# Chunk attention in front of a gated MLP on one core: norms moved behind PV, and PV and scores put in one place from unit 12

## The chip, the cores and the metric

The kernel runs on one core of a Trainium2 chip. The metric is the device time of one execution in microseconds (us); smaller is better. The time of a kernel is the median of several executions; one further view of it is a profiled execution, from which all rows of the profile come.

## The reference

```
q, k, v: (8, 8, 576, 64)  batch, heads, sequence, head_dim;  chunks of 64 positions
scores = q_c @ k_c.T / sqrt(64)             within each chunk of 64 alone
attn   = softmax(scores)
x      = (attn @ v_c) as (4608, 512)         tokens x (heads * head_dim)
h      = x @ w_in                            (4608, 2048)
out    = (h * sigmoid(beta * h)) @ w_out     (4608, 512), float32
```

## The kernel before

**Units and blocks.** The 4608 tokens are cut into 18 units of 256 tokens (two halves `s` of 128), and two units make one of nine blocks of 512 tokens, numbered 0 to 8. Attention works on units, the MLP on blocks. The kernel is one long list of instructions that is written out in the order in which each engine will run its share; nothing reorders it afterwards. Each engine runs its own instructions in that order and waits at one whose inputs or buffers aren't ready.

**The steps of a unit** u, with the lines of the profile:
- loads of q, k and v by GpSimd's DMA queue (L99, L113). The load of unit u + 4 is issued with T of unit u (`loads_to`), and waits until the buffers of unit u (four each for q and k) are free.
- `emit_T`: for units from 8 on, two DMA transposes on SP (L152), of k and then of q, into kT and qT, two buffers each.
- `emit_sc`: 32 small matmuls (64 x 64, L225) make the scores in the PSUM pool ps_s (one tile of two banks); ACT makes the exponential et (L231).
- `emit_pv`: for each half 16 small matmuls (64 x 65, L266), with a column of ones that gives the sum. Where they go is the argument `where`: "x" is the pool ps_x (one tile of two banks), "s" is ps_s, "p" two of the four banks of ps_p (the tiles called y).
- `emit_norm`: reciprocal (L285) and product (L287) on DVE, into x in 16 bits; for "p" in two parts.
- `emit_xt_dma`: one DMA transpose on SP (L318) into the xt tile of the block, which has three buffers. The first big matmul of a block needs all four transposes of its two units.

**The steps of a block** j: `emit_m` for m = 0 to 15: four matmuls of 128 x 512 (hps, L329) into one bank of ps_p, a tanh on ACT (sg, L339), and a product on DVE (gt, L343). `emit_t` for four tiles t of 128 tokens: 16 matmuls (ops, L361) into one bank of ps_p, in two halves of eight, then a copy on ACT (osb, L371) and the output by SP's DMA queue (L373). The four banks of ps_p are given out in turn to hps, ops and y tiles.

**The order.** For blocks 3 to 8 the order is made from a list of items with a position in the block (0 to 1) and a priority, and sorted by both. The m of block j stand at 0.02 + 0.061 m, the halves of t of block j - 1 at multiples of 0.1225, and between them the attention of the next block's units 2j + 2 and 2j + 3. There are two ways to place attention. Units below MU = 14 come through `att_items`: scores, T of the next unit, PV and the two norms stand at places of their own, in 0.43 of a block. Units from MU on come as a "hop": PV of the unit (its second half into ps_p), the scores of the next unit, T of the unit after that, and the norms with their transposes, all in one place. The scores of unit MU itself stand at 0.89 of the block before its hop.

Of the kernel before, what the change touches and what calls it, by code (L numbers as in the profile page):

```python
# [15 lines left out]
def kernel(  # L16
# [54 lines left out]
    blocks = [(u, 2) for u in range(0, NU, 2)]  # L71
    NB = len(blocks)
    XU = 8
    MU = 14
    unit_block = {}
    for j, (u0, n) in enumerate(blocks):
        for u in range(u0, u0 + n):
# [138 lines left out]
    def emit_sc(u, split=False, later=False):  # L216
        qt, kt = qT.pop(u), kT.pop(u)
        sc = ps_s.tile([128, 2, H, CH], FP32, tag="s", name="sc")
        if u >= XU:
            qx, kx = (t.rearrange("p h s e -> p (h s e)").rearrange("p (j c t) -> p j c t", j=H, c=2)  # L220
                      for t in (qt, kt))
            for jj in range(H):
                for par in range(2):
                    for c in range(2):
                        nc.tensor.matmul(  # L225
                            out=sc[64 * c:64 * c + 64, par, jj, :],
                            lhsT=kx[64 * par:64 * par + 64, jj, c, :],
                            rhs=qx[64 * par:64 * par + 64, jj, c, :],
                        )
            et = et_p.tile([128, 2, H, CH], FP16, tag="et", name="et")  # L230
            nc.scalar.activation(out=et, in_=sc, func=ACTF.Exp, scale=scale)  # L231
            et_t[u] = et
            return
        for h in range(H):
            for e in range(2):
                for c in range(4):
                    p0, o0 = 32 * c, 64 * (c % 2)
                    nc.tensor.matmul(  # L238
                        out=sc[o0:o0 + 64, c // 2, h, :],
                        lhsT=kt[p0:p0 + 32, h, :, e],  # L240
                        rhs=qt[p0:p0 + 32, h, :, e],
                        start=(e == 0),
                        stop=(e == 1),
                    )
        et = et_p.tile([128, 2, H, CH], FP16, tag="et", name="et")
        ex_t[u] = [
            lambda s=s: nc.scalar.activation(out=et[:, s], in_=sc[:, s], func=ACTF.Exp, scale=scale)  # L247
            for s in ([0, 1] if split or later else [slice(0, 2)])
        ]
        et_t[u] = et  # L250
        while ex_t[u] and not later:
            emit_ex(u)

    def emit_pv(u, where=("x", "s")):
        et = et_t.pop(u)
        for s in (1, 0) if u >= MU else (0, 1):
            i = 2 * u + s
# [17 lines left out]
    def emit_norms(u):  # L275
        for s in (1, 0) if u >= MU else (0, 1):
            emit_norm(u, s)
            emit_xt_dma(u, s)

    def emit_norm(u, s):  # L280
        x = x_t.pop((u, s))
        rd = rd_p.tile([128, 2, 4, 1], FP32, tag="rd", name="rd")
        x16 = x_p.tile([128, 2, 4, D], FP16, tag="x16", name="x16")
        for r, z in [(slice(0, 2), x[0])] if len(x) == 1 else list(enumerate(x)):
            nc.vector.reciprocal(out=rd[:, r], in_=z[..., D:D + 1])  # L285
            o = x16[:, r]
            nc.vector.tensor_tensor(  # L287
                out=o, in0=z[..., 0:D], in1=rd[:, r].to_broadcast(list(o.shape)), op=ALU.mult
            )
        x16_t[u, s] = x16  # L290
# [25 lines left out]
    def emit_xt_dma(u, s):  # L316
        xf = x16_t.pop((u, s)).rearrange("p r h d -> p (r h d)")
        nc.sync.dma_start_transpose(out=xt_at(u, s), in_=xf)  # L318
# [3 lines left out]
    def emit_m(j, m, c0=0, n=None, later=False):  # L322
        n = blocks[j][1] * UNIT if n is None else n
        if j not in gt_t:
            gt_t[j] = gt_p.tile([128, KFF, 512], FP16, tag="gt", name="gt")
        hps = ps_p.tile([128, 512], FP32, tag="p", name="hps")
        xr = xt_t[j].rearrange("p t (r k) (c q) -> p (t r) (k c) q", r=2, c=2)
        for kk in range(KDM):
            nc.tensor.matmul(  # L329
                out=hps[:, 0:n],  # L330
                lhsT=w_in16[m // 2][:, kk, (m % 2) * 128:(m % 2) * 128 + 128],
                rhs=xr[:, c0 // CH:(c0 + n) // CH, 2 * (kk % 2) + kk // 2, :],
                start=(kk == 0),
                stop=(kk == KDM - 1),
            )
        sg = sg_p.tile([128, 512], FP32, tag="sg", name="sg")

        def act():
            nc.scalar.activation(  # L339
                out=sg[:, 0:n], in_=hps[:, 0:n], func=ACTF.Tanh, scale=beta2[:, m:m + 1])  # L340

        def vec():
            nc.vector.scalar_tensor_tensor(  # L343
                out=gt_t[j][:, m, c0:c0 + n], in0=sg[:, 0:n], scalar=1.0, in1=hps[:, 0:n],
                op0=ALU.add, op1=ALU.mult,
            )

        if later:
            return act, vec
        act()  # L350
        vec()
# [3 lines left out]
    def emit_t(j, t, k0=0, k1=None):  # L355
        k1 = KFF if k1 is None else k1
        if k0 == 0:
            ops_t[j, t] = ps_p.tile([128, DM], FP32, tag="p", name="ops")
        ops = ops_t[j, t]
        for kk in range(k0, k1):  # L360
            nc.tensor.matmul(  # L361
                out=ops,
                lhsT=gt_t[j][:, kk, t * 128:(t + 1) * 128],
                rhs=w_out16[kk // 4][:, kk % 4, :],
                start=(kk == 0),
                stop=(kk == KFF - 1),
            )
        if k1 < KFF:
            return
        osb = osb_p.tile([128, DM], FP32, tag="osb", name="osb")  # L370
        nc.scalar.activation(out=osb, in_=ops, func=ACTF.Copy, scale=0.5)  # L371
        r0 = blocks[j][0] * UNIT + t * 128
        nc.sync.dma_start(out=out[r0:r0 + 128, :], in_=osb)  # L373
# [20 lines left out]
    with tc.manual_schedule():  # L394
# [74 lines left out]
        for i in range(16):  # L469
# [11 lines left out]
            if i == 15:  # L481
                a0, v0 = emit_m(1, 0, 0, 256, True)
# [74 lines left out]

        def att_items(u, a0, w):
            return [(a0, 2, ("sc", u)), (a0 + 0.40 * w, 3, ("pv", u)),
                    (a0 + 0.41 * w, 3, ("norm", u, 0)), (a0 + 0.55 * w, 3, ("norm", u, 1)),  # L560
                    (a0 + 0.10 * w, 3, ("T", u + 1))]

        for j in range(3, NB):
            items = [(0.02 + 0.98 * m / KFF, 0, ("m", m)) for m in range(KFF)]
            for t in range(4):
                for hf in range(2):
                    items.append((0.98 * (t + 0.5 * hf) / 4, 1, ("t", t, hf)))
            if 2 * j + 2 < MU:
                for i in range(2):
                    items += att_items(2 * j + 2 + i, 0.03 + 0.43 * i, 0.43)  # L570
                if 2 * j + 4 == MU:
                    items += [(0.89, 2, ("sc", MU)), (0.90, 3, ("T", MU + 1))]
            elif j + 1 < NB:
                for i in range(2):
                    items.append((0.15 + 0.5 * i, 2, ("hop", 2 * j + 2 + i)))
            items.sort(key=lambda it: it[:2])
            for _, _, it in items:
                if it[0] == "m":
                    emit_m(j, it[1])
                elif it[0] == "t":  # L580
                    emit_t(j - 1, it[1], 8 * it[2], 8 * it[2] + 8)
                elif it[0] == "sc":
                    emit_sc(it[1])
                elif it[0] == "pv":
                    emit_pv(it[1])
                elif it[0] == "hop":
                    emit_pv(it[1], ("x", "p" if it[1] + 1 < NU else "s"))
                    if it[1] + 1 < NU:
                        emit_sc(it[1] + 1)
                    if it[1] + 2 < NU:  # L590
                        emit_T(it[1] + 2)
                    emit_norms(it[1])
                elif it[0] == "norm":
                    emit_norm(it[1], it[2])
                    emit_xt_dma(it[1], it[2])
                elif it[1] < NU:
                    emit_T(it[1])
# [49 lines left out]
```

## Time and profile before

| | |
|---|---|
| median of 5 runs | 288.44 us (288.24, 288.29, 288.44, 289.51, 290.15) |
| profiled execution | 289.51 us, of which the span from first to last instruction is 287.7 |
| TensorE clock granted | 0.999 |
| busy: TensorE, ACT, DVE, GpSimd | 98%, 51%, 49%, 33% |
| big matmuls, hps (L329) and ops (L361) | 44% and 42% of the chain that ended last |
| transposes xt (L318), issue to landing | 2.4 to 7.3 us, median 3.5 |

Rows give the start, the duration, the engine, the line of the kernel and what is written and read (out<-in). A number in brackets is the idle time of the engine just before, with what ended it. "PEld" is TensorE's weight load, "SPq" an instruction that SP issues to its DMA queue. In the chain that ended last each piece follows on what released it; "issue" is time in which the engine waited for nothing that the profile shows.

### The profile page before, as it was taken

To read this page: it belongs to the slowest core of one execution; us is meant where nothing else is said; L and a number is where in the kernel's file an instruction comes from. 1 tells how busy PE (TensorE), PEld (TensorE's weight loads), DVE (VectorE), ACT (ScalarE), POOL (GpSimd) and SP (SyncE) were. 2 spreads that over 40 slices of the span, in tenths; PEclk is the share of its full clock that TensorE was granted. 3 is DMA by queue.
4 is the path that set the end of the run, shared out by engine and by line. 5 is a ranking of instruction groups with operands and counts; after the bars stand their busy time and mean duration, and the time that the engine had idled before them with its cause. 6 is when DMAs were issued, how large, how long until landed. Compare 5 with 4: busy or idle time off the path is not lost.

```text
span 287.7 us, 6664 instructions
## 1 busy us (share of the span) xinstructions
PE 280.6 (98%) x2779; PEld 136.2 (47%) x2779; DVE 141.9 (49%) x260; ACT 146.0 (51%) x223; POOL 95.7 (33%) x125
## 2 busy tenths in 40 slices
PE   6989999999999999999999999999999999999995
PEld 3464456544544444444444444444444444444444
DVE  3587533776558554535453445454544545333300
ACT  4377218773557545454544454554545444444411
POOL 8853677578073991243542600000000000000000
PEclk9999999999999999999999999999999999999999
DMA  8999999999999999999999992555451212010012
GB/s 198 177 197 206 181 179 210 209 161 152 198 100 175 177 176 179 131 173 114 174 147 170 132 191 60 127 76 127 57 129 39 73 39 73 36 39 36 36 73 75
DMA packets 141086, 37.40 MB, mean 130 GB/s; under 512 B 128001, under 2 KB 136577, under 8 KB 141057
## 3 DMA queue, kind: packets, MB, share of 16 engines
q0 software_dynamic: 99136, 17.83, 80.5%
q1 hardware_dynamic: 41776, 19.09, 30.8%
q8 instruction: 22, 0.36, 0.5%
q10 hardware_dynamic: 144, 0.07, 0.1%
q14 instruction: 8, 0.06, 0.1%
HBM read 36.71 MB, written 9.44 MB: 160 GB/s over the span
## 4 chain that ended last, share of the span: by engine, by line
PE 96%; POOL 1%; ACT 1%; issue 1%; DVE 0%; DVEq 0%; POOLq 0%
PE hps L329 44%; PE ops L361 42%; PE warm L381 2%; PE x L266 2%; PE sc L238 1%; PE sc L225 1%; PE ops L603 1%; ACT xt L304 1%; POOL h L401 1%; PE sc L198 1%; POOL vbig L113 1%; PE xp L303 0%; ACT et L208 0%; PE y L266 0%; PE xp L311 0%
## 5 line engine op out<-in xcount | busy, mean ns | idle before, releaser
L343 DVE SCALAR_TENSOR_TENSOR gt<-sg,hps 128x512 f16<-128x512 f32 (+1 forms) x153 | 99.2, 655 | 107.8 <-ACT sg L339 107.5
L329 PE MATMUL hps<-xt,win 128*128 128x512 f16 (+1 forms) x612 | 136.9, 367 | 1.3 <-ACT xt L304 0.7
L339 ACT ACTIVATE sg<-hps,beta 128x512 f32<-128x512 f32 (+1 forms) x153 | 100.4, 663 | 73.6 <-PE hps L329 73.5
L361 PE MATMUL ops<-wout,gt 128*128 128x512 f16 x560 | 131.1, 379 | 0.0
L329 PEld LDWEIGHTS <-win 128*128 128x128 f16 x612 | 58.0, 98 | 62.9 <-issue 2.0
L361 PEld LDWEIGHTS <-gt 128*128 128x128 f16 x560 | 54.0, 98 | 63.7
L371 ACT ACTIVATE osb<-ops 128x512 f32<-128x512 f32 x35 | 20.9, 598 | 42.5 <-PE ops L361 42.5
L113 POOL DMA_DIRECT2D vbig<-in_v_dram x40 | 34.3, 877 | 11.1 <-DMA wout<-in_moe_w_out_dram 3.2
L99 POOL DMA_DIRECT2D qu<-in_q_dram x22 | 18.8, 871 | 36.8 <-DMA qT<-qu 34.0
L287 DVE TENSOR_TENSOR x<-x,rd 128x512 f16<-128x512 f32 x31 | 21.4, 692 | 1.2
L99 POOL DMA_DIRECT2D ku<-in_k_dram x22 | 18.9, 889 | 0.0
L285 DVE RECIPROCAL rd<-x 128x8 f32<-128x8 f32 x31 | 6.2, 200 | 13.5 <-PE x L266 13.5
L247 ACT ACTIVATE et<-sc 128x1024 f16<-128x1024 f32 (+1 forms) x8 | 6.4, 811 | 8.7 <-PE sc L238 8.7
L231 ACT ACTIVATE et<-sc 128x1024 f16<-128x1024 f32 x10 | 10.2, 1018 | 0.2
L266 PEld LDWEIGHTS <-et 64*64 64x64 f16 x576 | 6.0, 107 | 7.4 <-issue 3.8
L381 PE MATMUL warm<-idle 128*128 128x512 f16 (+1 forms) x32 | 8.7, 425 | 0.0
L105 POOL DMA_DIRECT2D qu<-in_q_dram x9 | 6.8, 768 | 2.2 <-DMA win<-in_moe_w_in_dram 1.5
L266 PE MATMUL x<-vbig,et 64*64 64x65 f16 x496 | 7.3, 194 | 0.2 <-ACT et L208 0.2
L105 POOL DMA_DIRECT2D ku<-in_k_dram x9 | 6.8, 759 | 2.2 <-DMA win<-in_moe_w_in_dram 1.3
L615 DVE TENSOR_SCALAR osb<-ops 128x256 f32<-128x256 f32 (+1 forms) x2 | 0.7, 358 | 12.1 <-PE ops L603 12.1
L131 POOL DMA_DIRECT2D win<-in_moe_w_in_dram x8 | 6.0, 761 | 1.1 <-DMA vbig<-in_v_dram 1.1
L179 DVE STREAM_TRANSPOSE t<-h 128x512 f32<-128x512 f32 (+1 forms) x5 | 4.1, 905 | 3.3 <-ACT h L178 3.3
(46 smaller groups left out, 72.5 us busy)
## 6 DMA issues: line engine op xcount, KB each, us to landing
out_dram<-osb SPq DMA_DIRECT2D x35, 256.0 KB, 2.9
vbig<-in_v_dram POOLq DMA_DIRECT2D x32, 128.0 KB, 7.1
qu<-in_q_dram POOLq DMA_DIRECT2D x20, 128.0 KB, 4.9
ku<-in_k_dram POOLq DMA_DIRECT2D x20, 128.0 KB, 5.8
win<-in_moe_w_in_dram POOLq DMA_DIRECT2D x8, 256.0 KB, 8.7
wout<-in_moe_w_out_dram POOLq DMA_DIRECT2D x4, 512.0 KB, 12.7
qu<-in_q_dram POOLq DMA_DIRECT2D x3, 256.0 KB, 7.3
ku<-in_k_dram POOLq DMA_DIRECT2D x3, 256.0 KB, 7.8
```

The source lines that it names most:

```text
L99: nc.gpsimd.dma_start(out=tv[off:off + n, sp], in_=src[b, :, s:s + n, :].rearrange("h p d -> p h d"),)
L105: nc.gpsimd.dma_start(out=t[off // 2:(off + n) // 2], in_=src[b, :, s:s + n, :].rearrange("h (p r) d -> p h r d", r=2),)
L113: nc.gpsimd.dma_start(out=vbig[off:off + n, i, :, 0:D], in_=v[b, :, s:s + n, :].rearrange("h p d -> p h d"),)
L231: nc.scalar.activation(out=et, in_=sc, func=ACTF.Exp, scale=scale)
L266: nc.tensor.matmul(out=(x[0][64 * c:64 * c + 64, r, g, 0:D + 1] if len(x) == 1 else x[r][64 * c:64 * c + 64, g, 0:D + 1]), lhsT=(et[64 * r ...
L287: nc.vector.tensor_tensor(out=o, in0=z[..., 0:D], in1=rd[:, r].to_broadcast(list(o.shape)), op=ALU.mult)
L329: nc.tensor.matmul(out=hps[:, 0:n], lhsT=w_in16[m // 2][:, kk, (m % 2) * 128:(m % 2) * 128 + 128], rhs=xr[:, c0 // CH:(c0 + n) // CH, 2 * ...
L339: nc.scalar.activation(out=sg[:, 0:n], in_=hps[:, 0:n], func=ACTF.Tanh, scale=beta2[:, m:m + 1])
L343: nc.vector.scalar_tensor_tensor(out=gt_t[j][:, m, c0:c0 + n], in0=sg[:, 0:n], scalar=1.0, in1=hps[:, 0:n], op0=ALU.add, op1=ALU.mult,)
L361: nc.tensor.matmul(out=ops, lhsT=gt_t[j][:, kk, t * 128:(t + 1) * 128], rhs=w_out16[kk // 4][:, kk % 4, :], start=(kk == 0), stop=(kk == K ...
L371: nc.scalar.activation(out=osb, in_=ops, func=ACTF.Copy, scale=0.5)
L381: nc.tensor.matmul(out=d[:, 0:w], lhsT=idle[:, 0:128], rhs=idle[:, 0:w])
```

## The change

The norms of a unit below MU, and with them their xt transposes, now stand right behind its PV, both at the same position (before: the first just behind PV, the second 0.06 of a block later). MU is 12 instead of 14, so units 12 and 13 come as hops in block 5, and the scores of unit 12 and T of unit 13 stand at the end of block 4. The two hops of a block stand at 0.22 and 0.68 instead of 0.15 and 0.65. In `emit_pv` and `emit_norms` the halves of units from MU on go in the order 1, 0; this now holds for units 12 and 13 too.

```diff
-    MU = 14
+    MU = 12
...
             return [(a0, 2, ("sc", u)), (a0 + 0.40 * w, 3, ("pv", u)),
-                    (a0 + 0.41 * w, 3, ("norm", u, 0)), (a0 + 0.55 * w, 3, ("norm", u, 1)),
+                    (a0 + 0.40 * w, 4, ("norm", u, 0)), (a0 + 0.40 * w, 5, ("norm", u, 1)),
                     (a0 + 0.10 * w, 3, ("T", u + 1))]
...
-                    items.append((0.15 + 0.5 * i, 2, ("hop", 2 * j + 2 + i)))
+                    items.append((0.22 + 0.46 * i, 2, ("hop", 2 * j + 2 + i)))
```

In the list of each engine this does the following. On TensorE the scores of unit 12 stand between m 14 and m 15 of block 4 (before: between m 0 and m 1 of block 5); in block 5 there are two places with small matmuls instead of five; the first hop of blocks 5, 6 and 7 stands between m 3 and t 1 (before, in blocks 6 and 7: between m 2 and m 3), the second between m 10 and m 11 as before. On DVE the two norms of units 8 to 11 stand next to each other, ahead of the gt of the m that follows the PV (before: one m's gt ahead of the first, one between them). On SP the order is the same up to unit 12, and then T of 14 and 15 stand ahead of the xt transposes of 12 and 13. GpSimd's list is the same.

## The prediction

> **What bounds the kernel now.** I read the page's busy line first, then the waits of TensorE, then the chain in order of time around the blocks that are edited, and last the transposes there.
>
> ```profile
> PE 280.6 (98%) x2779; PEld 136.2 (47%) x2779; DVE 141.9 (49%) x260; ACT 146.0 (51%) x223; POOL 95.7 (33%) x125
> ```
>
> ```profile
> PE hps L329 <- issue: 0.5, 1, 0.5
> ```
>
> TensorE is busy 98% of the span, and DVE and ACT half of it. Behind the start, TensorE waits once, for 0.5 us. So an edit of order can gain only what lies between the big matmuls. The chain shows this price:
>
> ```profile
> 127.11 0.38 PE sc L225 x32
> 127.48 0.97 PE hps L329 x4
> ...
> 131.04 0.38 PE x L266 x32
> 131.42 0.97 PE hps L329 x4
> ...
> 154.07 1.73 PE ops L361 x8
> 155.80 0.50 issue
> 156.30 1.02 PE hps L329 x4
> ...
> 190.81 0.25 PE y L266 x16
> 191.19 0.32 PE sc L225 x32
> 191.50 0.97 PE hps L329 x4
> ...
> 242.90 1.73 PE ops L361 x8
> ...
> 270.53 10.36 PE ops L361 x48
> ```
>
> From 242.90 to 270.53 there are sixteen pieces of eight matmuls (8 pairs of m, 8 halves of t) and nothing else: 27.63 us is the bare block. Four hps matmuls are 0.86 us there; behind a small group they are 0.97.
>
> The 0.50 us at 155.80 is the first m of block 5. It needs the xt tile of block 5, the last piece of which is the second transpose of unit 11:
>
> ```profile
> L318 SPq DMA_TRANSPOSE xt<-x x1: 1190/1190/1190, 150.1 to 150.1; - x1
> DMA to landing us min/median/max: 6.2/6.2/6.2
> ```
>
> 150.1 + 6.2 = 156.3, where TensorE goes on. So this "issue" is a transpose that lands late.
>
> **Places on TensorE.** Block 4 runs from 124.52 to 154.07: 29.55 us, 1.92 over the bare block, for four places with a small group (sc 10, PV 10, sc 11, PV 11): 0.48 each. Block 6 runs from 184.77 to 213.99: 29.22 us, 1.59 over, for two hops: 0.80 each, with PV and scores together. Block 5 runs from 154.07 to 184.77: 30.70 us, 3.07 over. Its five places (sc 12, PV 12, sc 13, PV 13, sc 14) make 5 x 0.48 = 2.40, and 0.67 is left: 0.50 of idle time and 0.16 because the four matmuls behind it took 1.02 instead of 0.86.
>
> After the change sc 12 stands at the end of block 4 and hops 12 and 13 in block 5. Block 4 becomes 27.63 + 5 x 0.48 = 30.03, block 5 becomes 27.63 + 1.59 = 29.22 if nothing waits. Together 59.25 against 60.25: 1.00 us less, of which 0.33 comes from the places (five separate ones, 2.40, against one separate, 0.48, and two hops, 1.59) and 0.67 from the wait. No matmul is added or removed; blocks 6 and 7 keep their two hops.
>
> **Norms behind PV.** This is what takes the wait away. The timeline around the PV of unit 11, which ends at 145.33:
>
> ```profile
> 147.06 0.69 DVE L343 SCALAR_TENSOR_TENSOR gt<-sg,hps 128x512 f16<-128x512 f32 x1 [2.38 <-ACT sg L339]
> 147.66 0.20 DVE L285 RECIPROCAL rd<-x 128x8 f32<-128x8 f32 x1
> 147.90 0.69 DVE L287 TENSOR_TENSOR x<-x,rd 128x512 f16<-128x512 f32 x1
> 148.51 0.68 DVE L343 SCALAR_TENSOR_TENSOR gt<-sg,hps 128x512 f16<-128x512 f32 x1
> 148.62 2.63 SPq L318 DMA_TRANSPOSE xt<-x  x2
> ```
>
> DVE is idle for 2.38 us with the PV done, because the gt of m 10 stands ahead of the first norm in its order, and the gt of m 11 ahead of the second. So the transposes go out at 148.62 and 150.1. In the new order both norms stand ahead of the gt of m 10. A norm takes 0.93 (147.66 to 148.59); begun 0.2 after the PV (ACT's osb starts 0.2 behind its matmuls, 189.78 to 189.98), the two end at about 146.5 and 147.4, and the transposes can go out at about 146.5 and 147.7 (SP's issue of one takes 1.19): some 2.3 us earlier. Even at the 6.2 us of now the second lands at 154.0. The first m of block 5 will stand at 154.55 + 1.73 = 156.3, later than now because sc 12 (0.48) comes ahead of it. So there are 2.3 us of cover, and if it is gone the old 0.67 comes back.
>
> The page "DMA: Bandwidth & Descriptors" of the Trainium skill (section "Anatomy of one DMA") fits a transfer, for the GpSimd path, as about 2.0 us plus its bytes at 436 GB/s, which for the 128 KB of one xt transpose would make an estimate of 2.3 us. By that the transpose would land at 152.4, the wait would have another cause and stay, and only 0.33 would be gained. The trace has 2.4 to 2.5 us for the same transposes from 178 us on, but 4.4 to 7.3 while unit loads are in flight, so the row decides.
>
> What it costs: the gt of m 10 starts at 147.4 instead of 147.06, two norms having gone ahead, and ends at 148.1. Its PSUM bank is next wanted four ps_p tiles on, by m 13 at 149.75, so 1.6 us of room hide it; with the cover gone it would cost 0.3 at each of four units. I take nothing. Units 8, 9 and 10 change in the same way, without a wait to remove.
>
> **The hops of units 12 and 13.** In a hop the second half's PV goes into two of the four ps_p banks. In hop 14 of before this cost no wait (190.81 to 191.50). The page "TensorEngine Tiling (Array Packing)" of the Trainium skill (section "Gotcha 1: PSUM Pressure") warns that row tiling needs separate banks and so raises PSUM pressure. By it these banks would be missed by the big matmuls; the rows of hops 14 to 16 show no such wait, but the first hop's position is new, and that I work out next.
>
> **0.22 instead of 0.15.** The first hop of blocks 5, 6, 7 now stands after m 3, not after m 2. The second (0.68 for 0.65) stays between m 10 and m 11. Banks go round in fours: t 0, m 0, m 1, m 2, then m 3 takes t 0's, the two y tiles take those of m 0 and m 1 (free for long), and t 1 takes that of m 2. t 1 used to come one m later. In before the gt of m 2 ended 1.45 us after its matmuls (190.81 to 191.57 + 0.69). Now with the hop at T, m 2 ended at T - 0.86, its gt ends at T + 0.59, and t 1 is wanted at T + 0.70. That is 0.1 us of room. Below zero is excluded: the y tiles are now freed from waiting for osb of t 0, but TensorE's weight loads stand 0.42 idle ahead of them (released by ACT) just as they do ahead of the PV at 144.88, where nothing releases them. At the top I put one restart as seen at 156.30, 0.16, for each of three hops: 0 to 0.48. I take 0, as the rows fit.
>
> **T and SP.** In a hop T (u + 2) goes on SP ahead of the two xt transposes. T 14 moves from 169.5 to about 161.5, T 15 from 183.7 to about 176. Each pair of issues takes SP 2.5 to 4.5 us, then come the xt of 12 and 13, then outputs, of which four buffers exist. xt of 13 then go out about where hop 15 had them: PV 205.42, xt at 209.4 and 210.7, landing 2.5 later, 213.2, with the first m of the next block at 215.72. That is 2.5 us of room, and the same is left in block 5 (hop 13 at about 175.2). Unit loads on GpSimd wait for T: the last, unit 17, waits for T 13, which stays behind the last output of block 4 (153.5). T 13's own reader moves most: sc 13 goes from 169.5 to hop 12.
>
> **The sum.** Profiled execution: 289.51, less 1.00, is 288.51. It stands 1.07 over the median of the runs (288.44). The wait rests on loads and transposes that are paced by the same kernel, so I take it to be in the median run too: 288.44 - 1.00 = 287.44. An effect under 0.5% (1.44 us) can hardly be told from no change here, and this one is below that.
>
> **Rivals.** (1) Forecast: places and wait both go, 287.4 to 287.5. Chance 0.55.
> (2) The wait is not in the ordinary run, or something else ends it. For it speaks that the profiled execution is 1.07 longer than the median, more than the 0.67. Against: three of the five runs lie within 0.20, and nothing in the start reaches block 5 but through TensorE. Then only 0.33 goes: 288.1. Chance 0.2.
> (3) t 1 waits for the gt of m 2 in three blocks: 287.44 + 0.48 = 287.9. Chance 0.15.
> (4) Slower: sc 13 waits for its transposed q. The hop 12 stands at 154.55 + 4 x 1.73 = 161.5, sc 13 0.38 later at 161.85. T 13's second transpose goes out at 155.1 and took 5.1 us: 160.2, so 1.6 us of room where there were 9. With the 8.4 us that T 10 took it lands at 163.5; TensorE waits 1.65 and restarts for 0.16: 287.44 + 1.8 = 289.3, slower than before. It decides from a landing at 162.7 on (a wait of 0.84 plus 0.16 eats the 1.00), 7.6 us after issue. T 10 and T 11 took 8.4 and 7.9, T 12 5.9 and T 13 5.1 with the same loads around. Chance 0.1.
>
> **How the numbers follow.** The wait at block 5 could also be larger in other runs: a landing after 7.3 us, as the slowest xt took, is 1.1 later. So the low end goes to 286.8; the high end takes in rivals 2 and 3 with the spread of the runs, 288.8. Faster than 287.0 takes a larger wait removed: 0.14. Slower than 289.88 takes rival 4 with more than it has ever taken, or what I don't see: 0.07. The rest, 0.79, is within 0.5%.
>
> **What would show it.** Right: no idle TensorE at the start of block 5; block 4 at 30.0 and block 5 at 29.2; xt of unit 11 issued near 146.5 and 147.7; behind the first hops t 1 at once, eight matmuls in 1.83. Wrong: idle time ahead of sc 13 near 161.9 (rival 4), ahead of t 1 behind hops 12, 14, 16 (rival 3), or at the first m of block 6 near 185.5, where the xt of unit 13 would be late.

## The result, and the profile after

The changed kernel takes 288.26 us (median of 46 runs) against 289.13 us for the kernel before (88 runs by now). The ratio is 0.9971, with a 95% interval of 0.9963 to 0.9979: 0.84 us less, 0.61 to 1.07. The ratios here and below leave out executions more than 1.5% above the fastest of their kernel, of these 46 one of 292.80 us. The profiled execution took 287.84 us with a span of 286.0, against 289.51 and 287.7. Of this difference in span of 1.7 us, 0.80 had arisen before block 4 (which starts at 123.72 instead of 124.52), in a stretch that the change leaves nearly alone. The kernel before, profiled again further down, starts block 4 at 123.60, so this part belongs to the executions and not to the change.

The page of the changed kernel, busy line: TensorE is still the bound.

```profile
PE 279.3 (98%) x2779; PEld 136.2 (48%) x2779; DVE 143.0 (50%) x264; ACT 146.5 (51%) x223; POOL 95.8 (33%) x125
```

Its chain in order of time (start, duration, what), around the start of block 5 and its first hop:

```profile
151.54 0.86 PE hps L329 x4
152.41 0.38 PE sc L225 x32
152.78 0.97 PE hps L329 x4
153.75 1.73 PE ops L361 x8
155.48 1.73 PE hps L329 x8
...
160.66 0.25 PE y L266 x16
160.91 0.13 PE x L266 x16
161.03 0.32 PE sc L225 x32
161.35 1.83 PE ops L361 x8
...
182.97 1.73 PE ops L361 x8
```

The scores of unit 12 stand at 152.41, ahead of block 5. At 155.48 the first m of block 5 follows without the idle time. Block 4 takes 30.03 us (123.72 to 153.75), block 5 29.22 (to 182.97): together 59.25. Block 6 takes 29.25. Behind the hop, t 1 takes the bank that the gt of m 2 frees, and this gt ends 0.1 us ahead of it, at 161.24:

```profile
160.55 0.69 DVE L343 SCALAR_TENSOR_TENSOR gt<-sg,hps 128x512 f16<-128x512 f32 x1 [1.90 <-ACT sg L339]
```

Its timeline behind the PV of unit 11, which ends at 144.53:

```profile
144.46 0.21 DVE L285 RECIPROCAL rd<-x 128x8 f32<-128x8 f32 x1 [0.59 <-PE x L266]
144.70 0.69 DVE L287 TENSOR_TENSOR x<-x,rd 128x512 f16<-128x512 f32 x1
145.31 0.20 DVE L285 RECIPROCAL rd<-x 128x8 f32<-128x8 f32 x1
145.42 3.43 SPq L318 DMA_TRANSPOSE xt<-x  x2
```

The first norm starts as the PV ends, and the two transposes go out at 145.42 and 147.6. The view of the tile xt for the second one:

```profile
L318 SPq DMA_TRANSPOSE xt<-x x1: 1213/1213/1213, 147.6 to 147.6; - x1
DMA to landing us min/median/max: 5.2/5.2/5.2
```

It lands at 152.8, and its reader stands at 155.48: 2.7 us of cover.

### The profile page after: what moved, and what is told of

It is laid out like the page before. It is cut to its first block, busy times and chain, and to the rows that moved or that the text cites. A ratio compares the mean times of both kernels' runs of the same rounds, so it can differ in the third digit from the quotient of the medians.

```text
span 286.0 us, 6667 instructions
## 1 busy us (share of the span) xinstructions
PE 279.3 (98%) x2779; PEld 136.2 (48%) x2779; DVE 143.0 (50%) x264; ACT 146.5 (51%) x223; POOL 95.8 (33%) x125
## 4 chain that ended last, share of the span: by engine, by line
PE 96%; POOL 1%; ACT 1%; issue 1%; DVE 0%; DVEq 0%; POOLq 0%
PE hps L329 44%; PE ops L361 43%; PE x L266 2%; PE warm L381 2%; PE sc L238 1%; PE ops L603 1%; PE sc L225 1%; ACT xt L304 1%; POOL h L401 1%; PE y L266 1%; POOL vbig L113 1%; PE sc L198 0%; PE xp L303 0%; ACT et L208 0%; PE xp L311 0%
## 5 line engine op out<-in xcount | busy, mean ns | idle before, releaser
L287 DVE TENSOR_TENSOR x<-x,rd 128x512 f16<-128x512 f32 x29 | 20.1, 691 | 1.1
L381 PE MATMUL warm<-idle 128*128 128x512 f16 (+1 forms) x32 | 7.7, 391 | 0.0
L157 DVE STREAM_TRANSPOSE kT<-ku 128x512 f32<-128x512 f32 x6 | 4.2, 706 | 4.2 <-DMA ku<-in_k_dram 4.2
```

The costliest lines, as they stand in the source:

```text
L287: nc.vector.tensor_tensor(out=o, in0=z[..., 0:D], in1=rd[:, r].to_broadcast(list(o.shape)), op=ALU.mult)
L381: nc.tensor.matmul(out=d[:, 0:w], lhsT=idle[:, 0:128], rhs=idle[:, 0:w])
```

## Experiments: which part does what

Two theories. A: the places with small matmuls have a fixed price, and the wait at block 5 comes from the late transpose in every run. B: the wait was an accident of the one profiled execution, and only places count. The first four kernels take the change apart.

**Norms alone.**

```diff
-                    (a0 + 0.41 * w, 3, ("norm", u, 0)), (a0 + 0.55 * w, 3, ("norm", u, 1)),
+                    (a0 + 0.40 * w, 4, ("norm", u, 0)), (a0 + 0.40 * w, 5, ("norm", u, 1)),
```

> The kernel before with the norms behind PV and nothing else; MU stays 14, the hops at 0.15 and 0.65. Theory A (the late transpose of unit 11 makes the wait, in every run): the xt transposes of unit 11 go out some 2.3 us earlier, TensorE does not wait at the first m of block 5, block 5 is 27.63 + 5 x 0.48 = 30.0 us instead of 30.7, and the time is 0.67 us under before. Theory B (the wait was an accident of one execution): block 5 may be 30.0 us too, but the time does not differ from before.

Measured: no wait at block 5, which takes 30.03 us (153.57 to 183.60): 27.63 + 5 x 0.48. The first two pieces of block 5 in the chain, and the second xt transpose of unit 11:

```profile
153.57 1.73 PE ops L361 x8
155.30 0.86 PE hps L329 x4
```

```profile
L318 SPq DMA_TRANSPOSE xt<-x x1: 1220/1220/1220, 148.0 to 148.0; - x1
DMA to landing us min/median/max: 5.8/5.8/5.8
```

It lands at 153.8, 1.5 us ahead of its reader at 155.30; even the slowest landing met below, 7.1 us, would have been in time. The ratio is 0.9986 (0.9971 to 1.0001), about 0.4 us less; the interval reaches from nothing to more than the 0.67.

**MU alone.**

```diff
-    MU = 14
+    MU = 12
```

> The kernel before with MU = 12 and nothing else; norms and the hop positions as before. Theory A: the norms of unit 11 stay late, its second transpose lands some 6.2 us after issue, that is 31.75 us after the start of block 4; the first m of block 5 now stands 30.03 + 1.73 = 31.76 us after it, because the scores of unit 12 went ahead of it. So the wait is gone or under 0.3 us here too, and nearly the whole 1.00 us is gained without the norms. If instead the norms are what takes the wait away, block 5 keeps a wait of 0.5 and only 0.33 us is gained.

Measured: 0.9981 (0.9963 to 1.0), about 0.55 us less. The wait at the first m of block 5 is gone here too, but narrowly: the second transpose of unit 11 went out at 149.5 and landed 5.9 us later, some 0.3 us ahead of its reader, and a landing of 7.1 us would have been late. Another wait has come, in the waits of TensorE (total, times, longest):

```profile
PE sc L225 <- DMA qT<-qu: 0.5, 1, 0.5
```

These are the scores of unit 13 in hop 12, which stands at 0.15 here and meets the transposed q of unit 13. It is the slower rival of the prediction, and shows what 0.22 is good for: it moves this reader back by one m, 0.86 us.

**Hop positions alone.**

```diff
-                    items.append((0.15 + 0.5 * i, 2, ("hop", 2 * j + 2 + i)))
+                    items.append((0.22 + 0.46 * i, 2, ("hop", 2 * j + 2 + i)))
```

> The kernel before with the hops at 0.22 and 0.68 and nothing else; only the first hop of blocks 6 and 7 moves, behind m 3. Theory A: nothing, within 0.1 us; block 6 stays at 29.2 us, as t 1 has 0.1 us of room behind the hop. The rival that t 1 waits for the gt of m 2: up to 0.16 us for each of the two, and idle TensorE ahead of t 1. The wait at block 5 stays.

Measured: 1.001 (0.9989 to 1.0031), block 6 at 29.23 us, and t 1 follows the hop at once. But the wait at block 5, which nothing in this kernel should remove, is not there: the second transpose of unit 11 landed at 155.0, and its reader stands at 155.24.

**The kernel before, again.**

> The kernel before, profiled a second time. Theory A: block 5 again takes 30.5 to 30.9 us with a wait of about 0.5 us at its first m, ended by the second xt transpose of unit 11 about 6 us after its issue. Theory B: no such wait, block 5 at 30.0 us.

Measured: 288.06 us in its one execution, and in the chain this first m of block 5:

```profile
154.88 0.93 PE hps L329 x4
```

It took 0.93 instead of 0.86, so a wait of 0.07 us. The second transpose of unit 11 landed 5.6 us after issue, in the hop positions' kernel 5.5, in the first profile 6.2. Neither theory as stated holds: the path is as A says, but the landing varies from one execution to the next, and the reader stands just there. The next kernel was to take the loads away from these transposes.

**A later place for one load.**

```diff
-        if which[-1] == "qT" and u not in (6, 7, 8):
+        if which[-1] == "qT" and u not in (6, 7, 8, 12):
```

> The kernel before with one edit: T of unit 12 no longer issues the load of unit 16; T of unit 13 issues the loads of units 16 and 17 together. So no unit load is in flight while the xt transposes of unit 11 are. If the loads make the transpose late, it lands about 2.4 us after issue (the value in quiet), at 152.5 instead of 156.3, the wait at block 5 is gone and block 5 is 30.0 us. If the transposes of unit 12 or SP make it late, it stays near 6 us and the wait stays.

This missed its aim: GpSimd's order and waits stay the same, and the load of unit 16 still went out at 146.4 us. So it is one more execution of the kernel before, and a telling one, in the chain and in the view of xt:

```profile
155.34 1.44 issue
156.77 1.02 PE hps L329 x4
```

```profile
DMA to landing us min/median/max: 7.1/7.1/7.1
```

A wait of 1.44 us, with a landing of 7.1. Its time is that of before, 1.0008 (0.9981 to 1.0035).

**Loads held back.**

```diff
-        if which[-1] == "qT" and u not in (6, 7, 8):
+        if which[-1] == "qT" and u not in (6, 7, 8, 12, 13):
...
                     emit_norm(it[1], it[2])
+                    if it[1:] == (12, 1):
+                        emit_gate(12)
+                        loads_to(17)
                     emit_xt_dma(it[1], it[2])
```

> The kernel before with the loads of units 16 and 17 held back on GpSimd until the second norm of unit 12 is done (at about 165 us, by a copy of one element of its result), so that none is in flight while the xt transposes of unit 11 and T of unit 13 are. (Moving only the place of the load of unit 16 in the program had left GpSimd's order and waits as they were.) If the loads make the transposes late: the second xt of unit 11 lands 2.4 to 2.9 us after issue instead of 5.5 to 7.1, T of unit 13 in 3 to 4 us, no wait at block 5, block 5 at 30.0 us, and the time under before by the mean of the wait, about 0.5 us. If not, the landings stay at 5.5 to 7 us.

The view of xt for the two transposes of unit 11, and the timeline of TensorE later:

```profile
L318 SPq DMA_TRANSPOSE xt<-x x2: 1190/1194/1197, 148.7 to 150.1; - x2
DMA to landing us min/median/max: 2.4/2.4/2.4
```

```profile
186.73 1.90 PE L329 MATMUL hps<-xt,win 128*128 128x512 f16 x8 [0.84 <-DMA xt<-x]
...
192.75 0.45 PE L225 MATMUL sc<-qT,kT 64*64 64x64 f16 x32 [1.16 <-DMA qT<-qu]
```

With no load in flight the same transposes, issued at the same place, land in 2.4 us, where the four executions above with the old order had 3.7 to 7.1, and block 5 has no wait and takes 30.03 us. T of unit 13 landed in 3.1 and 3.3 us, as expected. So the loads are shown to be what delays them. The time was expected below that of before and is above it, 1.0046 (1.0022 to 1.0071): the held loads, issued from 167.5 us on, now stand beside the xt transposes of unit 13 (7.0 us to landing) and T of unit 15 (8.0 us), and TensorE waits 0.84 and 1.16 us for these.

**The price of a place.**

```diff
                     items.append((0.22 + 0.46 * i, 2, ("hop", 2 * j + 2 + i)))
+                    if 2 * j + 3 + i < NU:
+                        items.append((0.28 + 0.46 * i, 2, ("sc", 2 * j + 3 + i)))
...
-                    if it[1] + 1 < NU:
-                        emit_sc(it[1] + 1)
```

> The changed kernel, but the scores of the next unit stand at a place of their own, 0.06 of a block behind the hop; T, norms and PV stay in the hop. This measures the price of a place by itself. Theory A (0.48 for a separate place, 0.80 for a hop): 0.16 us more for each of five hops with scores, so blocks 5 and 6 take 29.55 us instead of 29.23, block 7 0.16 more, and the time is 0.8 us over the changed kernel. If places are free, it does not move.

Measured: blocks 5 and 6 take 30.19 and 30.18 us, 0.97 and 0.93 more, for two hops with scores each, and the ratio to before is 1.0045 (1.0023 to 1.0067), some 2.1 us above the changed kernel's. That is 0.47 to 0.48 for each pair, not 0.16. The timeline gives the rest:

```profile
161.76 0.69 DVE L343 SCALAR_TENSOR_TENSOR gt<-sg,hps 128x512 f16<-128x512 f32 x1 [1.90 <-ACT sg L339]
...
162.50 1.89 PE L361 MATMUL ops<-wout,gt 128*128 128x512 f16 x8 [0.26 <-DVE gt L343]
```

A hop without scores is 0.32 us shorter, and now t 1 waits for the gt of m 2 that holds its bank (161.76 + 0.69 = 162.45): 0.26 us idle, and in the chain eight matmuls in 1.89 behind it instead of the 1.83 behind a hop. These 0.32 us are the wait, and 0.16 is left for the place, as the blocks of before had it. It is rival 3, provoked, and it shows the room the prediction had worked out: the gt ends 0.6 us behind the end of m 3, and the scores in the hop are what covers it. The place alone was not measured apart from it.

**The slower rival, provoked.**

```diff
-                    items.append((0.22 + 0.46 * i, 2, ("hop", 2 * j + 2 + i)))
+                    items.append(((0.08 if (i, j) == (0, 5) else 0.22) + 0.46 * i, 2, ("hop", 2 * j + 2 + i)))
```

> The changed kernel with the first hop of block 5 at 0.08 instead of 0.22, behind m 0. This provokes the slower rival of the prediction: scores of unit 13 now stand about 3.0 us after the start of block 5, while their transposed q lands 5.0 to 6.0 us after it. Expected: TensorE waits 1.5 to 2.5 us ahead of the scores of unit 13 and restarts for 0.16, block 5 takes 30.9 to 32 us instead of 29.2. If T of unit 13 is not what bounds it, block 5 stays at 29.2.

The timeline, and the busy time by stretch (behind POOL's, the granted clock, DMA's share and GB/s):

```profile
160.81 0.64 PE L225 MATMUL sc<-qT,kT 64*64 64x64 f16 x32 [3.26 <-DMA qT<-qu]
161.38 1.89 PE L329 MATMUL hps<-xt,win 128*128 128x512 f16 x4
163.07 2.43 PE L361 MATMUL ops<-wout,gt 128*128 128x512 f16 x8
```

```profile
161.00:162.00 1.00, 1.00 (x34) 0.60 (x27) 0.00 (x0) 0.50 (x1) 0.80 (x1) 0.50 1.08 204
163.00:164.00 1.00, 1.00 (x4) 0.38 (x3) 0.00 (x0) 0.69 (x1) 1.00 (x2) 0.50 4.79 41
165.00:166.00 1.00, 1.00 (x7) 0.41 (x5) 0.00 (x0) 0.47 (x1) 1.00 (x2) 1.00 2.20 154
```

The q of unit 13 landed at 160.7, 5.6 us after issue, and TensorE waited 3.26 us. Behind that the granted clock is 0.50 up to about 164 us: four hps matmuls take 1.8 us instead of 0.9. Block 5 takes 34.2 us, which is 29.2, the wait and some 1.7 of the low clock: 5.0 more, where 1.7 to 2.8 were expected. The ratio is 1.0106 (1.0062 to 1.0151), and the ten executions lie between 289.67 and 298.71 us.

**The changed kernel again.**

> The changed kernel a second time. If the wait at block 5 is a matter of chance in the kernel before (0.50, 0.07, 0 and 1.44 us in four executions of it or of kernels equal to it up to there) and has 2.7 us of cover in the changed one, there is none here again: blocks 4 and 5 together take 59.25 us within 0.05, and the time is 0.3% under before.

Measured: 288.41 us against 288.78, 0.9985 (0.9952 to 1.0017). The profiled execution took 292.12 us. It has no wait at the first m of block 5, but this in the timeline, and then a low clock in the busy time by stretch:

```profile
163.62 0.44 PE L225 MATMUL sc<-qT,kT 64*64 64x64 f16 x32 [2.13 <-DMA qT<-qu]
```

```profile
167.00:168.00 1.00, 1.00 (x4) 0.30 (x2) 0.00 (x0) 0.00 (x0) 1.00 (x2) 0.50 1.06 67
```

The second transpose of T 13 went out at 154.73 and took 8.8 us. Blocks 4 and 5 took 63.2 us and not 59.25: 2.13 of waiting and some 1.8 of the low clock. So the slower rival does occur in the changed kernel. The median hardly shows it, but in the mean the changed kernel lost here: five of these 12 executions took 291.9 to 294.2 us, where none of the 28 of the kernel before beside them was above 290.9, and the means are 290.04 against 288.92. Only one of the five was profiled, so that the others have the same cause is not shown.

**Further in the same direction.** MU = 10:

```diff
-    MU = 12
+    MU = 10
```

> The changed kernel with MU = 10: units 10 and 11 come as hops in block 4 too. Places: 0.33 us less. But T of unit 11 goes out while loads are in flight (it took 7.9 to 8.2 us), so its q lands about 8.5 to 9 us after the start of block 4, where the scores of unit 11 stand at 7.3: a wait of 1.2 to 1.7 us and a restart. And the xt transposes of unit 11 now stand behind T of unit 13 on SP and go out some 4 us after their PV: landing about 32 us after the start of block 4, where the first m of block 5 stands at 30.9, so another wait of about 1. Expected: 1 to 2.5 us slower than the changed kernel. If only places count, 0.33 us faster.

Measured: 290.14 us, 1.0033 (1.0004 to 1.0063), 1.9 us over the changed kernel. TensorE waits 1.7 us for the q of unit 11, and block 4 takes 31.09 us (125.07 to 156.16) instead of the 29.22 of two hops; the second wait, at block 5, did not come, as the xt of unit 11 landed at 156.0 with its reader at 157.9. The same with an earlier T:

```diff
-                    items += [(0.89, 2, ("sc", MU)), (0.90, 3, ("T", MU + 1))]
+                    items += [(0.80, 2, ("sc", MU)), (0.81, 3, ("T", MU + 1))]
```

> The kernel with MU = 10 in which TensorE waited 1.7 us for the transposed q of unit 11, but with the scores of unit MU at 0.80 and T of the next at 0.81 of the block before, instead of 0.89 and 0.90. T of unit 11 stands ahead of one output on SP then and can go out some 3.7 us earlier. If the landing of T 11 is all that makes MU = 10 slow, no wait is left, block 4 takes 29.2 us, and the time is 0.33 us under the changed kernel. If units 10 and 11 as hops cost more than that (xt of unit 11 behind T of unit 13 on SP, late for block 5), a wait of up to 1 us shows at the first m of block 5.

Measured: the wait for the q of unit 11 is gone, but the xt of unit 11, queued behind T 13 on SP, went out at 152.8 and landed 6.7 us later, and TensorE waited 4.6 us at block 5. The ratio is 1.0069 (1.0036 to 1.0102). The wait is read in one execution, of 295.11 us; the median of all twelve is 292.91. Neither the gain of 0.33 nor the wait of up to 1 us that were expected came. Last, the same early T with MU = 12:

> The changed kernel with the scores of unit 12 at 0.80 and T of unit 13 at 0.81 of block 4 instead of 0.89 and 0.90: T of unit 13 then stands ahead of one output on SP and goes out right behind the xt transposes of unit 11, some 3 us earlier, while its reader, the scores of unit 13 in hop 12, stays where it is. If a late T of unit 13 is what now and then makes the changed kernel wait (2.1 us in one execution, with the granted clock below 1 behind it), no execution is over 290 us and none has a mean clock under 0.998; the median stays within 0.1% of the changed kernel. If T of unit 13 now collides with the load of unit 16 and lands no earlier, the late executions stay.

Measured: 288.25 us, 0.9972 (0.9951 to 0.9992): the changed kernel's time, not better. T 13 went out at 149.05 and 150.38, but among the loads of unit 16, and its q took 7.2 us: it landed at 157.6 with its reader at 160.9, no more room than in the changed kernel's own profile (157.7 and 161.03). None of the 12 executions was above 289.9 us, but this kernel ran on another chip than the one on which five of 12 were long, so whether it takes the long ones away stays open.

## Why the prediction was right, and where it was not

- **Places.** Blocks 4 and 5 were to take 30.03 and 29.22 us, and did: 30.03 and 29.22. Where nothing waits, blocks 4 and 5 of the old order take 29.55 and 30.03, so the places are worth the 0.33 us forecast.
- **The wait.** The cause (a transpose of unit 11 that lands late among unit loads) and its end were right: with the loads held back it lands in 2.4 us and block 5 has no wait, and with the norms behind PV it is in time even with the slowest landing seen. The scores of unit 12 ahead of its reader add only 0.48 us, which was enough in one execution and need not be in others. Mis-sized was the step "so I take it to be in the median run too". Its idle time was 0.50, 0.07, 0 and 1.44 us in four executions with the old order there, since the landing varies from 5.5 to 7.1 us. With the restart of 0.16 behind the two long ones the mean is (0.66 + 0.07 + 0 + 1.60) / 4 = 0.58. With 0.33 this makes 0.91 us, against 0.84 measured (0.61 to 1.07) and 1.00 forecast. Rival 2 thus held for two of the four. How the wait is spread over many executions isn't known from four, and a mean of four stands here beside a difference of medians, so that 0.91 and 0.84 lie so close is in part luck.
- **The base.** The 287.44 us was counted from five executions of the kernel before, with a median of 288.44; over 88 it is 289.13. So the difference was met within 0.16 us, but the time itself is 0.82 above the forecast, 0.69 of it from the base. The low end of the range doesn't follow from the reason given for it: a landing 1.1 us later would make 287.44 - 1.1 = 286.3 and not 286.8.
- **The page's 2.3 us** for a transfer of this size agrees with 2.4 in quiet and not with the 4.0 to 7.1 that the second transpose of unit 11 took among loads, and it is the second that the sum had to be made with. The prediction read 4.4 to 7.3 among loads; the kernel before has 3.4 there too, at 167.5 us.
- **Norms.** The first transpose was to go out 1.2 us behind the PV and the second 2.4; they went out at 0.9 and 3.1, as SP's issue of the first took 2.1 us and not 1.2. The cover was forecast at 2.3 us and is 2.7 in this profile, by luck: the landing took 5.2 us, and with the 6.2 that the prediction counted the cover would be 1.7.
- **0.22.** t 1 follows at once with the 0.1 us of room that was worked out (161.24 to 161.35). Without the scores in the hop the room is gone.
- **The slower rival.** It exists (waits of 0.5 us with the hop at 0.15, 3.26 at 0.08, and once 2.13 at 0.22). The prediction counted on a landing 5.1 us after issue and put the turn at 7.6; the two profiled executions of the changed kernel had 3.6 and 8.8. Its price was too low: behind waits of more than 2 us the clock fell as well.

## What to carry to other kernels

A wait on the bound engine in one profiled execution is a sample: before its length goes into a sum, ask how far its transfer's landing varies and where its reader stands within that spread. Collecting small matmuls in one place saves little on TensorE (0.16 us a pair here), and each such move pulls readers towards their transposes, so the positions have to be set by the landing times under load, and judged by the long executions as well as by the median. Work that starts a transfer belongs ahead of work that only frees a buffer with room to spare.

## What the runs showed of the hardware that was not expected

The second xt transpose of unit 11, 128 KB, lands in 2.4 us in quiet and in 4.0 to 7.1 us while GpSimd's loads are in flight. And a wait of TensorE can cost more than itself. The granted clock fell to 0.50 for some 3.4 us near the end of the wait of 3.26 us, and for some 6.8 us near the end of that of 4.6 us. With the wait of 2.13 us it fell 1.5 us after TensorE had gone on, to 0.50 for some 3.4 us. After waits of 1.44 and 1.7 us it stayed at 1.00. The page "TensorE: Matmul & The Clock Gate" of the Trainium skill (section "Why this matters for your kernels") warns of gaps above some 3 us; in this one execution 2.13 us, just behind the 0.4 us of small matmuls of a PV, were enough.
